# A recurrent attention and feed-forward kernel: reordering the load-and-multiply setup and spreading the feed-forward weight loads over the first steps

## The chip, the cores and the metric

The kernel runs on one core of one Trainium2 chip. The metric is the device time of one execution in microseconds (us), the median of several. Engines: PE is TensorE, DVE is VectorE, ACT is ScalarE, POOL is GpSimd, SP is the engine whose queue issues most of the loads.

## The reference

Two layers with the same weights are applied, each one attention block and one feed-forward block. Attention walks over 64 segments of 32 tokens, one after the other; each segment also sees 8 memory rows that the segment before it produced.

```python
x = x + A(layernorm(x));  x = x + B(layernorm(x))      # twice, same weights

def A(x, mem, Wq, Wk, Wv, Wo):          # 16 heads of 256, model width 448
    for s in range(64):                 # each segment needs the one before
        h = concat(mem, x[32*s : 32*s+32])              # 40 rows
        q, k, v = h @ Wq, h @ Wk, h @ Wv                # per head
        p = softmax(where(mask, q @ k.T / 16, -1e9))
        o = concat_heads(p @ v) @ Wo
        mem, out = o[:8], o[8:]

def B(x):                               # 448 -> 1792 -> 448
    g = x @ W_gate
    return (relu(g) * (x @ W_up)) @ W_down
```

## The kernel before

The kernel never computes q, k and v. In a setup stage it multiplies the weights with each other, per head: M = Wk·Wq (used for the scores) and B = Wv·Wo (used for the values). Then it runs 70 steps; in each, layer 1 handles one segment and layer 2 the segment six steps behind. The feed-forward work is filled into the steps from step 4 on.

K, Q and V arrive through a DMA that transposes on the way. One load of K, Q or V brings 1024 columns, which is four heads, 0.92 MB.

```python
def load_T(n, i):
    t = bp.tile([P, 8, DM], BF, tag=f"w{n}", name=f"w{n}")        # two buffers of each
    nc.sync.dma_start_transpose(t[:], srcs[n][:, 1024 * i:1024 * (i + 1)])
    return t

for i in range(4):                       # M: four groups of four heads
    wk, wq = load_T("k", i), load_T("q", i)
    for hh in range(4):
        for mt in range(3):
            product(ps[:, 0:DM], wk, wq, hh, 128 * mt, 128)       # 2 matmuls of 448 columns
            store_M(...)                                          # copies on ACT and DVE in turn
    ...
nc.sync.dma_start(x_ring[:, 1:R, :], ...)
for i in range(4):                       # B: four groups of four heads
    wv = load_T("v", i)
    nc.sync.dma_start(wo[:], WoF[:, 8 * i:8 * (i + 1), :])
    ...                                                           # same products and copies
nc.sync.dma_start(Wd_sb[:], B_W_down...)                          # 1.6 MB, first used in step 4
...
for half, w in zip(HALVES, (B_W_gate, B_W_up)):                   # 3.2 MB, first used in step 4
    nc.sync.dma_start(Wgu[half], w.rearrange("(c p) n -> p c n", p=64))
```

Only PE's instructions are pinned to program order, and only after the setup. The order of the load queue and of DVE is left to the scheduler. A step, cut to what matters:

```python
def step(g, inG, mid, before, late, end, last):
    # gps: 28 tiles of M x h for even and odd heads, evicted to G by ACT and DVE
    # S_ps: scores = h x G;  mid(): feed-forward work as filler
    vm.both(True)          # values of the memory and of part of the rows, tail rows of B
    # scores -> max, exp (ACT), sum, reciprocal, weights Px / Pm (DVE)
    vm.both(False)         # values, the other rows of B; here PE hides the softmax
    turn_P()               # transposes of the weights on PE
    # AT_ps: weights x values -> mb -> new memory rows (mps) into hTr: the next step waits for these
    nc.sync.dma_start(ys[...], mb[...])       # y<-mb: output rows to where layer 1 adds them up
```

Of the kernel before, what the change touches and what calls it, by code (L numbers as in the profile page):

```python
# [9 lines left out]
BF = mybir.dt.bfloat16  # L10
# [40 lines left out]
def build_kernel(ctx, tc, A_x, A_mem0, A_Wq, A_Wk, A_Wv, A_Wo, B_W_gate, B_W_up, B_W_down, out,  # L51
# [12 lines left out]
    nc.sync.dma_start(x_ring[:, 0, :], x_dram[0:128])  # L64
# [17 lines left out]
    Wd_sb = glob.tile([P, FT, DM], BF)  # L82
# [25 lines left out]
    with tc.tile_pool(name="bpre", bufs=2) as bp:  # L108
        maskf = bp.tile([P, L], F32, bufs=1)
        nc.gpsimd.memset(maskf[:], 0.0)  # L110
        nc.gpsimd.affine_select(
            out=maskf[0:SEG, 0:SEG], in_=maskf[0:SEG, 0:SEG],
            compare_op=ALU.is_ge, fill=MASKVAL, base=0,
            pattern=[[-1, SEG]], channel_multiplier=1,
        )
        nc.vector.memset(maskb[:], 0.0)
        for half in HALVES:
            nc.vector.tensor_copy(maskb[half], maskf[LO].unsqueeze(1).to_broadcast([64, 8, L]))

        srcs = {n: w.rearrange("d h e -> d (h e)") for n, w in (("k", A_Wk), ("q", A_Wq), ("v", A_Wv))}  # L120
        WoF = A_Wo.rearrange("h (t p) d -> p (h t) d", p=P)

        def load_T(n, i):
            t = bp.tile([P, 8, DM], BF, tag=f"w{n}", name=f"w{n}")
            nc.sync.dma_start_transpose(t[:], srcs[n][:, 1024 * i:1024 * (i + 1)])  # L125
            return t

        flip = [0]

        def copy_out(dst, src):  # L130
            flip[0] ^= 1
            if flip[0]:
                nc.scalar.copy(dst, src)
            else:
                nc.vector.tensor_copy(dst, src)

        def product(dst, lt, rt, hh, lo, n):
            for t in range(2):
                nc.tensor.matmul(dst, lt[:, 2 * hh + t, lo:lo + n], rt[:, 2 * hh + t, :],  # L139
                                 start=(t == 0), stop=(t == 1))  # L140

        def store_M(dst, odd, ps):
            if not odd:
                copy_out(dst[:, 0:448], ps)
            else:
                copy_out(dst[:, 512:896], ps[:, 0:384])
                copy_out(dst[:, 448:512], ps[:, 384:448])

        for i in range(4):
            wk = load_T("k", i)  # L150
            wq = load_T("q", i)
            for hh in range(4):
                o = 896 * ((4 * i + hh) // 2)
                for mt in range(3):
                    ps = psum.tile([P, 512], F32, tag="ps")
                    product(ps[:, 0:DM], wk, wq, hh, 128 * mt, 128)
                    store_M(M_sb[:, mt, o:o + 896], hh % 2, ps[:, 0:DM])
            for e in range(2):
                ps = psum.tile([P, 512], F32, tag="ps")
                for side in range(2):  # L160
                    product(ps[64 * side:64 * side + 64, 0:DM], wk, wq, 2 * side + e, 384, 64)
                store_M(MT_sb[:, 896 * i:896 * i + 896], e, ps[:, 0:DM])
        if R > 1:
            nc.sync.dma_start(x_ring[:, 1:R, :], x_dram[128:R * 128].rearrange("(t p) d -> p t d", p=P))
        for i in range(4):
            wv = load_T("v", i)
            wo = bp.tile([P, 8, DM], BF, tag="wo", name="wo")
            nc.sync.dma_start(wo[:], WoF[:, 8 * i:8 * (i + 1), :])
            for hh in range(4):
# [46 lines left out]
    for q in PTs:  # L216
        nc.gpsimd.memset(q[:], 0.0)
# [369 lines left out]
    def none():  # L587
        pass
# [120 lines left out]
```

## Time and profile before

| | before |
|---|---|
| median of 5 runs | 1640.02 us (1639.82 to 1641.61) |
| setup, until step 0's first `gps` matmul | 80.28 us, PE busy 51.51 us |
| step 0 | 25.39 us |
| steps 1 and 2 | 15.25 and 15.83 us |

The page's overview cuts the span into 40 equal slices of about 41 us and gives for each the busy share in tenths. The DMA row is the mean busy share of the 16 DMA engines.

```profile
PE   5778999999999999999999999999999999999997
...
PEclk8989999999999999999999999999999999999999
DMA  9830000000000000000000000000000000000000
```

PE is the bound from the fifth slice on. Only in the first four slices is PE partly idle (besides the very end), above all in the first three, and the DMA engines are 80% busy or more in the first two of them and nearly unused from the fourth on. So the setup and step 0 are the place to look at. The next view is the stage table. Each line is: stretch, its length, busy us and instruction count of PE, PEld (weight loads), DVE, ACT and POOL, then granted clock, DMA share and GB/s.

```profile
core 0: us, PE busy (x) PEld busy (x) DVE busy (x) ACT busy (x) POOL busy (x), PEclk, DMA share, GB/s
0.00:80.28 80.28, 51.51 (x269) 23.65 (x270) 40.34 (x90) 31.92 (x72) 6.04 (x23) 0.89 0.95 212
80.28:105.67 25.39, 17.98 (x397) 12.06 (x397) 9.05 (x22) 5.74 (x14) 3.57 (x8) 0.80 0.65 128
105.67:120.92 15.25, 12.64 (x336) 9.58 (x336) 7.04 (x17) 4.47 (x11) 0.45 (x2) 1.00 0.02 5
120.92:136.75 15.83, 14.91 (x396) 10.64 (x396) 7.91 (x18) 5.19 (x13) 0.45 (x2) 1.00 0.02 5
```

Two facts stand out. In setup the DMA engines are 0.95 busy and PE only 64%. Step 0 does the same work as step 2 and takes 9.6 us longer. The timeline of PE tells where it stands still (start, duration, engine, line, operation, operands, count, and in brackets the idle time before it and what ended it):

```profile
11.18 7.49 PE L139 MATMUL ps<-wq,wk 128*128 128x448 bf16 x32 [11.18 <-DMA wq<-in_A_Wq_dram]
...
33.65 13.72 PE L139 MATMUL ps<-wq,wk 128*128 128x448 bf16 x64 [8.39 <-DMA wq<-in_A_Wq_dram]
...
66.42 12.71 PE L139 MATMUL ps<-wo,wv 128*128 128x448 bf16 x64 [6.56 <-DMA wo<-in_A_Wo_dram]
80.28 0.57 PE L193 MATMUL gps<-hTr,MT_sb 64*128 64x40 bf16 x32 [0.41 <-DVE hTr L260]
90.44 0.45 PE L193 MATMUL gps<-hTr,MT_sb 64*128 64x40 bf16 x16 [5.06 <-issue]
```

Three long waits in setup end with a weight load. The last line is different: for 5.06 us PE waits for nothing that the profile names ("issue"). The DMA view of the six microseconds before 87 us, and then of the one microsecond that follows, gives a hint. Its lines are: queue, kind, packets, MB, share of the 16 engines.

```profile
q1 hardware_dynamic: 350, 1.25, 98.9%
```

```profile
q1 hardware_dynamic: 52, 0.19, 97.8%
q8 instruction: 1, 0.02, 8.7%
```

From 81 to 87 us the gate and up weights fill the engines and not one packet of instructions comes through. Between 87 and 88 us one begins. In the trace this packet holds 16,384 bytes and takes from 87.5 to 88.9 us, and PE goes on at 90.4.

### The profile page before, as it was taken

How to read it: one execution, taken by the hardware profiler on the slowest of the kernel's cores; microseconds unless marked ns; L12 is line 12 of the kernel's file. 1: busy time of each engine (PE TensorE's matmuls, PEld its weight loads, DVE VectorE, ACT ScalarE, POOL GpSimd, SP SyncE). 2: the span in 40 equal slices, each digit the busy share in tenths (PEclk: the TensorE clock that was granted, in tenths of full speed). 3: DMA queues.
4: the chain of work that ended last, by engine and by line, in shares of the span. 5: the costliest groups of instructions: out<-in, count | busy, mean ns of one | idle time of the engine just before them, and what ended most of it. 6: DMA issues, size and time to landing. Idle time of an engine off the chain costs nothing.

```text
span 1638.1 us, 82234 instructions
## 1 busy us (share of the span) xinstructions
PE 1566.3 (96%) x38680; PEld 1176.4 (72%) x38680; DVE 946.0 (58%) x2074; ACT 634.4 (39%) x1430; POOL 140.3 (9%) x370
## 2 busy tenths in 40 slices
PE   5778999999999999999999999999999999999997
PEld 2356767777777777777777777777778777777775
DVE  4634556565566665655656666665655666555553
ACT  2522333444334343434434443434334443434342
POOL 1000011000011010100101100010010100000000
PEclk8989999999999999999999999999999999999999
DMA  9830000000000000000000000000000000000000
GB/s 219 202 78 5 5 6 6 7 5 12 7 11 7 10 7 11 7 6 11 6 12 6 11 6 12 7 8 10 4 12 7 8 7 7 6 9 6 7 5 9
DMA packets 61348, 32.12 MB, mean 20 GB/s; under 512 B 46024, under 2 KB 60112, under 8 KB 61008
## 3 DMA queue, kind: packets, MB, share of 16 engines
q1 hardware_dynamic: 60976, 26.85, 7.1%
q8 instruction: 302, 4.95, 1.3%
q14 instruction: 38, 0.31, 0.1%
q10 hardware_dynamic: 32, 0.01, 0.0%
HBM read 10.33 MB, written 1.84 MB: 7 GB/s over the span
## 4 chain that ended last, share of the span: by engine, by line
PE 83%; DVE 9%; DMA 3%; SPq 2%; issue 1%; POOL 1%; ACT 1%; POOLq 0%; DVEq 0%; ACTq 0%
PE gps L193 27%; PE vps L193 23%; PE gate L193 10%; PE AT_ps L193 7%; PE S_ps L193 6%; PE dps L193 5%; PE PT_ps L196 2%; SPq L125 2%; PE ps L139 1%; DVE Px L471 1%; PE tps L196 1%; DMA y<-mb 1%; DVE ssum L463 1%; DVE vox L353 1%; DVE se L459 1%
## 5 line engine op out<-in xcount | busy, mean ns | idle before, releaser
L193 PE MATMUL gps<-hTr,M_sb 128*128 128x80 bf16 (+1 forms) x11760 | 418.2, 198 | 0.2
L193 PEld LDWEIGHTS <-M_sb 128*128 128x128 bf16 x11760 | 406.3, 99 | 5.0 <-issue 0.5
L401 DVE CAST G<-gps 128x480 bf16<-128x480 f32 (+3 forms) x326 | 190.7, 611 | 218.5 <-PE gps L193 217.7
L193 PEld LDWEIGHTS <-hTr 128*32 128x32 bf16 (+3 forms) x7936 | 197.8, 96 | 147.6 <-issue 40.7
L401 ACT CAST G<-gps 128x480 bf16<-128x480 f32 (+3 forms) x326 | 165.5, 526 | 339.9 <-PE gps L193 339.9
L193 PE MATMUL vps<-B_sb,hTr 128*32 128x448 bf16 x4608 | 242.6, 354 | 0.0
L193 PE MATMUL gate<-xnT,Wgu 64*128 64x128 bf16 x3136 | 206.4, 218 | 1.0 <-ACT xnT L278 1.0
L193 PE MATMUL up<-xnT,Wgu 64*128 64x128 bf16 x3136 | 206.9, 218 | 0.3 <-issue 0.3
L193 PEld LDWEIGHTS <-Wgu 64*128 64x128 bf16 x6272 | 185.2, 95 | 19.5 <-issue 12.7
L193 PE MATMUL vps<-B_sb,memTp 128*32 128x448 bf16 x3360 | 171.7, 353 | 0.0
L353 ACT CAST vox<-vps 128x448 bf16<-128x448 f32 x192 | 99.3, 533 | 175.1 <-PE vps L193 175.1
L353 ACT CAST VOm<-vps 128x448 bf16<-128x448 f32 x210 | 103.5, 526 | 144.2 <-PE vps L193 144.1
L193 PEld LDWEIGHTS <-memTp 128*32 128x32 bf16 (+1 forms) x4480 | 98.4, 95 | 80.0 <-issue 2.2
L353 DVE CAST vox<-vps 128x448 bf16<-128x448 f32 x192 | 116.9, 622 | 56.3 <-PE vps L193 55.2
L291 DVE SCALAR_TENSOR_TENSOR hh<-gate,ut 128x256 bf16<-128x256 f32 x224 | 94.7, 423 | 74.1 <-ACT ut L290 71.4
L193 PEld LDWEIGHTS <-PT 128*64 128x64 bf16 x2048 | 96.9, 110 | 40.2 <-issue 13.7
L290 ACT CAST ut<-up 128x256 bf16<-128x256 f32 x224 | 83.3, 372 | 101.1 <-PE up L193 78.7
L193 PE MATMUL AT_ps<-VOm,PT 128*64 128x320 bf16 (+1 forms) x1280 | 98.4, 262 | 1.3 <-DVE PT L503 1.3
L193 PE MATMUL gps<-hTr,MT_sb 64*128 64x80 bf16 (+1 forms) x3920 | 91.1, 195 | 8.1 <-issue 5.1
L458 DVE TENSOR_REDUCE mx<-S_ps 104x8 f32<-104x320 f32 (+1 forms) x140 | 62.2, 486 | 60.3 <-PE S_ps L193 60.3
L193 PE MATMUL dps<-Wd_sb,hh 128*128 128x448 bf16 x448 | 92.6, 353 | 0.0
L193 PEld LDWEIGHTS <-MT_sb 64*128 64x128 bf16 x3920 | 76.3, 96 | 18.5 <-issue 12.5
(83 smaller groups left out, 1420.9 us busy)
## 6 DMA issues: line engine op xcount, KB each, us to landing
wo<-in_A_Wo_dram SPq DMA_DIRECT2D x4, 896.0 KB, 6.1
y<-mb SPq DMA_DIRECT2D x128, 28.0 KB, 1.8
out_dram<-x_ring SPq DMA_DIRECT2D x16, 112.0 KB, 1.7
Wd_sb<-in_B_W_down_dram SPq DMA_DIRECT2D x1, 1568.0 KB
Wgu<-in_B_W_gate_dram SPq DMA_DIRECT2D x1, 1568.0 KB, 11.8
Wgu<-in_B_W_up_dram SPq DMA_DIRECT2D x1, 1568.0 KB, 18.2
x_ring<-in_A_x_dram SPq DMA_DIRECT2D x11, 112.0 KB, 2.1
x_ring<-in_A_x_dram SPq DMA_DIRECT2D x1, 560.0 KB, 5.1
```

Of the source, the lines that this page charges most:

```text
L125: nc.sync.dma_start_transpose(t[:], srcs[n][:, 1024 * i:1024 * (i + 1)])
L139: nc.tensor.matmul(dst, lt[:, 2 * hh + t, lo:lo + n], rt[:, 2 * hh + t, :], start=(t == 0), stop=(t == 1))
L193: in_order(nc.tensor.matmul(*a, **k))
L196: in_order(nc.tensor.transpose(*a))
L290: nc.scalar.copy(ut[:], gu[1][:])
L291: nc.vector.scalar_tensor_tensor(out=self.hh[:, f:f + 2, :], in0=gu[0][:], scalar=0.0, in1=ut[:], op0=ALU.max, op1=ALU.mult)
L353: self.evac[2 * x + e](self.dst[:, 2 * e + x, :], self.ps[x][e][:, 0:DM])
L401: (cp_a, cp_v)[self.side](G[:, self.side, self.t0:self.t0 + self.n, c0:c1, :], self.ps[:, 0:self.n * NP].rearrange("p (m c t) -> p m c t", ...
L458: nc.vector.tensor_reduce(mx[RR, e], S3, axis=AX.X, op=ALU.max)
L459: nc.vector.tensor_tensor(se[RR, 8 * e:8 * e + 8], S3, mx[RR, e].unsqueeze(2).to_broadcast([nr, 8, L]), op=ALU.subtract)
L463: nc.vector.tensor_reduce(ssum[RR, :], se[RR], axis=AX.X, op=ALU.add)
L471: eng.tensor_tensor(dst, se[rr, :, lo:hi], rs[rr, :].unsqueeze(2).to_broadcast([n, H, hi - lo]), op=ALU.mult)
```

## The change: its intent and the diff

The intent is to keep PE supplied during setup and to take everything out of setup that step 0 does not need. The core of the diff:

```diff
+        # in_order: one chain for each engine, used for the load queue and DVE's setup copies too
-        if pe_last[0] is not None:
-            tc.add_manual_dep(op.ins, pe_last[0], ...)
-        pe_last[0] = op.ins.name
+        eng = op.ins.engine
+        if eng in last_of:
+            tc.add_manual_dep(op.ins, last_of[eng], ...)
+        last_of[eng] = op.ins.name
...
+    def load_vo(j):                       # two heads at a time, V as it lies in memory
+        if j >= 6: ...                    # the last two pairs: V by the transposing DMA, as before
+        w, cols = wvn[j % 2], slice(512 * j, 512 * j + 512)
+        in_order(nc.sync.dma_start(w[:, 0:3, :], srcs["v"][0:384, cols].rearrange("(c p) e -> p c e", p=P)))
+        in_order(nc.sync.dma_start(w[LO, 3, :], srcs["v"][384:448, cols]))
+        in_order(nc.sync.dma_start(wo[:], WoF[:, 4 * j:4 * (j + 1), :]))
...
+    def turn_B(j):                        # 16 transposes on PE, copies of 128x896 on ACT and DVE
+    def mul_B(j):                         # the products of two heads
+    def make_B(j): turn_B(j); mul_B(j)
...
+    load_vo(0); load_vo(1); load_kq(0)
+    make_B(0); load_vo(2); make_B(1); load_vo(3); load_kq(1)
+    make_M(0); load_kq(2)
+    ...                                   # memory rows, first two x tiles
+    for j in (2, 3): make_B(j); load_vo(j + 2)
+    make_M(1); load_kq(3); make_M(2)
+    for j in (4, 5): make_B(j); load_vo(j + 2)
+    ...                                   # other x tiles
+    make_M(3)
...
+        if g == 0:                        # step 0 takes the last two products
+            def mid():  mul_B(6)
+            def soft(): mul_B(7); late_pools()
...
+    # late_pools: gate and up weights in 14 pieces, Wd in 7 (224 KB each), queued in `loads`
+    def load_when(op):                    # issue the next piece once op is done
+        if loads:
+            dma = nc.sync.dma_start(*loads.popleft())
+            tc.add_manual_dep(dma.ins, op.ins.name, ...)
+    # called at DVE's evictions of G, at both exponentials and at both copies of PT
```

More of the change, by code (lines that the diff above doesn't have):

```diff
@@ L63, in build_kernel @@
     x_ring = glob.tile([P, R, DM], BF)
-    nc.sync.dma_start(x_ring[:, 0, :], x_dram[0:128])
+    nc.sync.dma_start(x_ring[:, 0:2, :], x_dram[0:256].rearrange("(t p) d -> p t d", p=P))
     def xsl(t):
@@ L81, in build_kernel @@
     BT_sb = glob.tile([P, H // 2, DM], BF)
-    Wd_sb = glob.tile([P, FT, DM], BF)
     hTr = glob.tile([P, NR, NSL, 2, L], BF)
@@ L106, in build_kernel @@
     psum = ctx.enter_context(tc.tile_pool(name="psum", bufs=8, space=bass.MemoryType.PSUM))
-    with tc.tile_pool(name="bpre", bufs=2) as bp:
-        maskf = bp.tile([P, L], F32, bufs=1)
-        nc.gpsimd.memset(maskf[:], 0.0)
-        nc.gpsimd.affine_select(
-            out=maskf[0:SEG, 0:SEG], in_=maskf[0:SEG, 0:SEG],
-            compare_op=ALU.is_ge, fill=MASKVAL, base=0,
-            pattern=[[-1, SEG]], channel_multiplier=1,
-        )
-        nc.vector.memset(maskb[:], 0.0)
-        for half in HALVES:
-            nc.vector.tensor_copy(maskb[half], maskf[LO].unsqueeze(1).to_broadcast([64, 8, L]))
-        srcs = {n: w.rearrange("d h e -> d (h e)") for n, w in (("k", A_Wk), ("q", A_Wq), ("v", A_Wv))}
-        WoF = A_Wo.rearrange("h (t p) d -> p (h t) d", p=P)
-        def load_T(n, i):
-            t = bp.tile([P, 8, DM], BF, tag=f"w{n}", name=f"w{n}")
-            nc.sync.dma_start_transpose(t[:], srcs[n][:, 1024 * i:1024 * (i + 1)])
-            return t
-        flip = [0]
-        def copy_out(dst, src):
-            flip[0] ^= 1
-            if flip[0]:
-                nc.scalar.copy(dst, src)
-            else:
-                nc.vector.tensor_copy(dst, src)
-        def product(dst, lt, rt, hh, lo, n):
-            for t in range(2):
-                nc.tensor.matmul(dst, lt[:, 2 * hh + t, lo:lo + n], rt[:, 2 * hh + t, :],
-                                 start=(t == 0), stop=(t == 1))
-        def store_M(dst, odd, ps):
-            if not odd:
-                copy_out(dst[:, 0:448], ps)
-            else:
-                copy_out(dst[:, 512:896], ps[:, 0:384])
-                copy_out(dst[:, 448:512], ps[:, 384:448])
-        for i in range(4):
-            wk = load_T("k", i)
-            wq = load_T("q", i)
-            for hh in range(4):
-                o = 896 * ((4 * i + hh) // 2)
-                for mt in range(3):
-                    ps = psum.tile([P, 512], F32, tag="ps")
-                    product(ps[:, 0:DM], wk, wq, hh, 128 * mt, 128)
-                    store_M(M_sb[:, mt, o:o + 896], hh % 2, ps[:, 0:DM])
-            for e in range(2):
-                ps = psum.tile([P, 512], F32, tag="ps")
-                for side in range(2):
-                    product(ps[64 * side:64 * side + 64, 0:DM], wk, wq, 2 * side + e, 384, 64)
-                store_M(MT_sb[:, 896 * i:896 * i + 896], e, ps[:, 0:DM])
-        if R > 1:
-            nc.sync.dma_start(x_ring[:, 1:R, :], x_dram[128:R * 128].rearrange("(t p) d -> p t d", p=P))
-        for i in range(4):
-            wv = load_T("v", i)
-            wo = bp.tile([P, 8, DM], BF, tag="wo", name="wo")
-            nc.sync.dma_start(wo[:], WoF[:, 8 * i:8 * (i + 1), :])
-            for hh in range(4):
-                h = 4 * i + hh
-                for mt in range(3):
-                    ps = psum.tile([P, 512], F32, tag="ps")
-                    product(ps[:, 0:DM], wv, wo, hh, 128 * mt, 128)
-                    copy_out(B_sb[:, mt, place(h), :], ps[:, 0:DM])
-            for pair in range(2):
-                ps = psum.tile([P, 512], F32, tag="ps")
-                for e, half in enumerate(HALVES):
-                    product(ps[half, 0:DM], wv, wo, 2 * pair + e, 384, 64)
-                copy_out(BT_sb[:, place(4 * i + 2 * pair), :], ps[:, 0:DM])
-        nc.sync.dma_start(Wd_sb[:], B_W_down.rearrange("(f p) d -> p f d", p=P))
@@ L182, in build_kernel @@
-    pe_last = [None]
+    last_of = {}
     def in_order(op):
-        if pe_last[0] is not None:
-            tc.add_manual_dep(op.ins, pe_last[0],
+        eng = op.ins.engine
+        if eng in last_of:
+            tc.add_manual_dep(op.ins, last_of[eng],
                               mybir.DependencyInfo(mybir.DependencyClass.NoSync, mybir.DependencyReason.DATA),
                               reason="in_order")
-        pe_last[0] = op.ins.name
+        last_of[eng] = op.ins.name
     def matmul(*a, **k):
@@ L196, in transpose @@
         in_order(nc.tensor.transpose(*a))
-    pa = ctx.enter_context(tc.tile_pool(name="pa", bufs=1))
     p_vo = ctx.enter_context(tc.tile_pool(name="p_vo", bufs=1))
     p_soft = ctx.enter_context(tc.tile_pool(name="p_soft", bufs=1))
-    p_fb = ctx.enter_context(tc.tile_pool(name="p_fb", bufs=2))
-    p_y = ctx.enter_context(tc.tile_pool(name="p_y", bufs=2))
-    Wgu = pa.tile([P, NCH, F], BF)
-    for half, w in zip(HALVES, (B_W_gate, B_W_up)):
-        nc.sync.dma_start(Wgu[half], w.rearrange("(c p) n -> p c n", p=64))
+    p_pp = ctx.enter_context(tc.tile_pool(name="p_pp", bufs=1))
     PXM = []
     for i in range(2):
-        pp = [pa.tile([P, H, SEG], BF, name=f"P{n}{i}") for n in "xm"]
+        pp = [p_pp.tile([P, H, SEG], BF, name=f"P{n}{i}") for n in "xm"]
         for q in pp:
@@ L213, in build_kernel @@
         PXM.append(pp)
-    xnTs = [pa.tile([P, NCH, P], BF, name=f"xnT{i}") for i in range(2)]
-    PTs = [pa.tile([P, 8, P], BF, name=f"PT{i}") for i in range(2)]
+    PTs = [p_pp.tile([P, 8, P], BF, name=f"PT{i}") for i in range(2)]
     for q in PTs:
         nc.gpsimd.memset(q[:], 0.0)
+    bpre = ExitStack()
+    bp = bpre.enter_context(tc.tile_pool(name="bpre", bufs=2))
+    wvn = [bp.tile([P, NSL, 512], BF, name=f"wvn{i}", bufs=1) for i in range(2)]
+    for w in wvn:
+        nc.vector.memset(w[HI, 3], 0.0)
@@ new lines, in build_kernel @@
+    maskf = bp.tile([P, L], F32, bufs=1)
+    nc.gpsimd.memset(maskf[:], 0.0)
+    nc.gpsimd.affine_select(
+        out=maskf[0:SEG, 0:SEG], in_=maskf[0:SEG, 0:SEG],
+        compare_op=ALU.is_ge, fill=MASKVAL, base=0,
+        pattern=[[-1, SEG]], channel_multiplier=1,
+    )
+    nc.vector.memset(maskb[:], 0.0)
+    for half in HALVES:
+        nc.vector.tensor_copy(maskb[half], maskf[LO].unsqueeze(1).to_broadcast([64, 8, L]))
+    srcs = {n: w.rearrange("d h e -> d (h e)") for n, w in (("k", A_Wk), ("q", A_Wq), ("v", A_Wv))}
@@ new lines, in build_kernel, with load_T, load_kq @@
+    WoF = A_Wo.rearrange("h (t p) d -> p (h t) d", p=P)
+    def load_T(n, i):
+        t = bp.tile([P, 8, DM], BF, tag=f"w{n}", name=f"w{n}")
+        in_order(nc.sync.dma_start_transpose(t[:], srcs[n][:, 1024 * i:1024 * (i + 1)]))
+        return t
+    kq, vo, turned = {}, {}, {}
+    def load_kq(i):
+        kq[i] = load_T("k", i), load_T("q", i)
+    def load_vo(j):
+        if j >= 6:
+            if j == 6:
+                kq["v"] = bp.tile([P, 8, DM], BF, tag="wk", name="wk")
+                in_order(nc.sync.dma_start_transpose(kq["v"][:], srcs["v"][:, 3072:4096]))
+            wo = bp.tile([P, 4, DM], BF, tag="wo", name="wo")
+            in_order(nc.sync.dma_start(wo[:], WoF[:, 4 * j:4 * (j + 1), :]))
+            turned[j] = kq["v"][:, 4 * (j - 6):4 * (j - 6) + 4], wo
+            return
+        w, cols = wvn[j % 2], slice(512 * j, 512 * j + 512)
+        in_order(nc.sync.dma_start(w[:, 0:3, :], srcs["v"][0:384, cols].rearrange("(c p) e -> p c e", p=P)))
+        in_order(nc.sync.dma_start(w[LO, 3, :], srcs["v"][384:448, cols]))
+        wo = bp.tile([P, 4, DM], BF, tag="wo", name="wo")
+        in_order(nc.sync.dma_start(wo[:], WoF[:, 4 * j:4 * (j + 1), :]))
+        vo[j] = w, wo
@@ new lines, in build_kernel, with copy_out, product, store_M @@
+    flip = [0]
+    def copy_out(dst, src):
+        flip[0] ^= 1
+        if flip[0]:
+            nc.scalar.copy(dst, src)
+        else:
+            in_order(nc.vector.tensor_copy(dst, src))
+    def product(dst, lt, rt, hh, lo, n):
+        for t in range(2):
+            matmul(dst, lt[:, 2 * hh + t, lo:lo + n], rt[:, 2 * hh + t, :], start=(t == 0), stop=(t == 1))
+    def store_M(dst, odd, ps):
+        if not odd:
+            copy_out(dst[:, 0:448], ps)
+        else:
+            copy_out(dst[:, 512:896], ps[:, 0:384])
+            copy_out(dst[:, 448:512], ps[:, 384:448])
@@ new lines, in make_M @@
+    def make_M(i):
+        wk, wq = kq.pop(i)
+        for hh in range(4):
+            o = 896 * ((4 * i + hh) // 2)
+            for mt in range(3):
+                ps = psum.tile([P, 512], F32, tag="ps")
+                product(ps[:, 0:DM], wk, wq, hh, 128 * mt, 128)
+                store_M(M_sb[:, mt, o:o + 896], hh % 2, ps[:, 0:DM])
+        for e in range(2):
+            ps = psum.tile([P, 512], F32, tag="ps")
+            for side in range(2):
+                product(ps[64 * side:64 * side + 64, 0:DM], wk, wq, 2 * side + e, 384, 64)
+            store_M(MT_sb[:, 896 * i:896 * i + 896], e, ps[:, 0:DM])
@@ new lines, in make_B @@
+    def make_B(j):
+        turn_B(j)
+        mul_B(j)
+    def turn_B(j):
+        wn, wo = vo.pop(j)
+        wv = bp.tile([P, 4, DM], BF, tag="wv", name="wv")
+        for a in range(2):
+            tp = psum.tile([P, 2, 512], BF, tag="ps", name="tp")
+            for b in range(2):
+                for dc in range(NSL):
+                    transpose(tp[:, b, 128 * dc:128 * dc + 128],
+                              wn[:, dc, 128 * (2 * a + b):128 * (2 * a + b) + 128], ident[:])
+            copy_out(wv[:, 2 * a:2 * a + 2, :], tp[:, :, 0:DM])
+        turned[j] = wv, wo
@@ new lines, in mul_B @@
+    def mul_B(j):
+        wv, wo = turned.pop(j)
+        ps = psum.tile([P, 512], F32, tag="ps")
+        for e, half in enumerate(HALVES):
+            product(ps[half, 0:DM], wv, wo, e, 384, 64)
+        copy_out(BT_sb[:, place(2 * j), :], ps[:, 0:DM])
+        for hh in range(2):
+            for mt in range(3):
+                ps = psum.tile([P, 512], F32, tag="ps")
+                product(ps[:, 0:DM], wv, wo, hh, 128 * mt, 128)
+                copy_out(B_sb[:, mt, place(2 * j + hh), :], ps[:, 0:DM])
@@ L222, in ln @@
         stats = p_ln.tile([P, nc.vector.BN_STATS_DIM], F32, tag="ln_stats")
-        nc.vector.bn_stats(stats[:], xt)
+        (in_order if t >= 2 else (lambda op: None))(nc.vector.bn_stats(stats[:], xt))
         mv = p_ln.tile([P, nc.vector.BN_AGGR_DIM], F32, tag="ln_mv")
@@ L275, in turn @@
                 transpose(tps[:, k], self.xn[:, k].rearrange("p a b -> p (a b)"), ident[:])
-            self.xnT = xnTs[n_xn[1] % 2]
+            self.xnT = late_sb["xnT"][n_xn[1] % 2]
             n_xn[1] += 1
             nc.scalar.copy(self.xnT[:], tps[:])
-            self.hh = p_fb.tile([P, FT, P], BF, tag="hh", name="hh")
+            self.hh = late_sb["fb"].tile([P, FT, P], BF, tag="hh", name="hh")
         def gate_up(self, f):
@@ L286, in gate_up @@
                     for half, ps in zip(HALVES, gu):
-                        matmul(ps[:, ff], Wgu[half, k, col], self.xnT[half, k],
+                        matmul(ps[:, ff], late_sb["Wgu"][half, k, col], self.xnT[half, k],
                                          start=(k == 0), stop=(k == NCH - 1))
-            ut = p_fb.tile([P, 2, P], BF, tag="ut")
+            ut = late_sb["fb"].tile([P, 2, P], BF, tag="ut")
             nc.scalar.copy(ut[:], gu[1][:])
@@ L298, in down @@
             for f in range(lo, hi):
-                matmul(ps[:, 0:DM], self.hh[:, f, :], Wd_sb[:, f, :], start=(f == 0), stop=(f == FT - 1))
+                matmul(ps[:, 0:DM], self.hh[:, f, :], late_sb["Wd"][:, f, :], start=(f == 0), stop=(f == FT - 1))
             if hi < FT:
@@ L357, in both, with late_pools @@
             self.part(1, tail)
+    late_sb = {}
+    ys = {}
+    loads = deque()
+    def late_pools():
+        bpre.close()
+        pa = ctx.enter_context(tc.tile_pool(name="pa", bufs=1))
+        late_sb["fb"] = ctx.enter_context(tc.tile_pool(name="p_fb", bufs=2))
+        late_sb["y"] = ctx.enter_context(tc.tile_pool(name="p_y", bufs=2))
+        late_sb["xnT"] = [pa.tile([P, NCH, P], BF, name=f"xnT{i}") for i in range(2)]
+        Wgu = late_sb["Wgu"] = pa.tile([P, NCH, F], BF, name="Wgu")
+        Wd = late_sb["Wd"] = pa.tile([P, FT, DM], BF, name="Wd")
+        for k in range(NCH):
+            for half, w in zip(HALVES, (B_W_gate, B_W_up)):
+                loads.append((Wgu[half, k], w[64 * k:64 * k + 64, :]))
+        for f in range(0, FT, 2):
+            loads.append((Wd[:, f:f + 2, :], B_W_down[128 * f:128 * f + 256, :].rearrange("(f p) d -> p f d", p=P)))
+    def load_when(op):
+        if loads:
+            dma = nc.sync.dma_start(*loads.popleft())
+            tc.add_manual_dep(dma.ins, op.ins.name,
+                              mybir.DependencyInfo(mybir.DependencyClass.Sync, mybir.DependencyReason.DATA),
+                              reason="load_when")
     prev_vom = [None]
@@ L361, in build_kernel, with step @@
     cp_v = nc.vector.tensor_copy
-    def step(g, inG, mid, before, late, end, last):
+    def step(g, inG, mid, soft, before, late, end, last):
         chains = [c for c in (C1, C2) if 0 <= g - c.lag < nseg]
@@ L400, in out @@
             def out(self):
-                (cp_a, cp_v)[self.side](
+                op = (cp_a, cp_v)[self.side](
                     G[:, self.side, self.t0:self.t0 + self.n, c0:c1, :],
                     self.ps[:, 0:self.n * NP].rearrange("p (m c t) -> p m c t", m=self.n, t=L))
+                if self.side:
+                    load_when(op)
         def pair_of_banks(k):
@@ L438, in step @@
         vm = Values(lambda rr, k: memTp[g % 2][rr, k, :], VOm, [cp_a, cp_v, cp_a, cp_a])
-        vm.both(True)
+        if g:
+            vm.both(True)
         for c in chains:
@@ L460, in step @@
                                     mx[RR, e].unsqueeze(2).to_broadcast([nr, 8, L]), op=ALU.subtract)
-            nc.scalar.activation(se[RR, 8 * e:8 * e + 8], se[RR, 8 * e:8 * e + 8], AF.Exp, scale=SCALE)
+            load_when(nc.scalar.activation(se[RR, 8 * e:8 * e + 8], se[RR, 8 * e:8 * e + 8], AF.Exp, scale=SCALE))
         ssum = p_soft.tile([P, H], F32, tag="ssum")
@@ L502, in turn_P @@
                     transpose(PT_ps[:, g4, RR], Pt[RR, 4 * g4:4 * g4 + 4, :], ident[RR, RR])
-                cp(PT[:, gg:gg + 4, RR], PT_ps[:, :, RR])
+                load_when(cp(PT[:, gg:gg + 4, RR], PT_ps[:, :, RR]))
             late()
+        soft()
+        if not g:
+            vm.both(True)
         vm.both(False)
@@ L562, in step @@
             if j == 0:
-                ys[c.cid] = p_y.tile([P, DM], BF, tag=f"y{c.cid}", name="y")
+                ys[c.cid] = late_sb["y"].tile([P, DM], BF, tag=f"y{c.cid}", name="y")
             nc.sync.dma_start(ys[c.cid][32 * j:32 * j + 32, :], mb[c.rb:c.rb + SEG, 0:DM])
@@ L567, in step @@
         last()
-    ys = {}
     xn_of = {}
@@ L578, in prep_pe, with none @@
             prep_x(c, t, xn_of.pop((c.cid, t)))
+    def none():
+        pass
+    load_vo(0)
+    load_vo(1)
+    load_kq(0)
+    make_B(0)
+    load_vo(2)
+    make_B(1)
+    load_vo(3)
+    load_kq(1)
+    make_M(0)
+    load_kq(2)
     tps0 = transposed(mem_in, MEM)
@@ L585, in build_kernel @@
         prep_pe(C1, t)
-    def none():
-        pass
+    for j in (2, 3):
+        make_B(j)
+        load_vo(j + 2)
+    make_M(1)
+    load_kq(3)
+    make_M(2)
+    for j in (4, 5):
+        make_B(j)
+        load_vo(j + 2)
+    if R > 2:
+        in_order(nc.sync.dma_start(x_ring[:, 2:R, :], x_dram[256:R * 128].rearrange("(t p) d -> p t d", p=P)))
+    make_M(3)
     nc.gpsimd.tensor_copy(memTp[0][:, :, 0:16], hTr[:, 1, :, 0, 0:16])
@@ L594, in build_kernel, with mid, soft, end @@
             set_mem0(C2)
-        inG = mid = before = late = end = last = none
-        if r == 0:
+        inG = mid = soft = before = late = end = last = none
+        if g == 0:
+            def mid():
+                mul_B(6)
+            def soft():
+                mul_B(7)
+                late_pools()
+            def end():
+                prep_ln(C1, gb + 2)
+        elif r == 0:
             def inG():
@@ L647, in last @@
                 fill(1, 1)
-        step(g, inG, mid, before, late, end, last)
+        step(g, inG, mid, soft, before, late, end, last)
         for c in (C1, C2):
```

## The prediction

> **What bounds it now.** Overall TensorE: the page has PE at 96% of the span, and the chain of waits is 83% PE. The steady part (192.7 to 1600 us, PE 98.8% busy) is barely touched; the change concerns the first 106 us. The stage table gives: setup 0 to 80.28 us, PE busy 51.5 us, DMA share 0.95; step 0 from 80.28 to 105.67, that is 25.4 us, where steps 1 and 2 take 15.3 and 15.8 us.
>
> In setup PE stands still for about 28 us (timeline): 11.2 us for the first turned weights, 8.4 us (25.3 to 33.6) for the third pair, 6.5 us (60 to 66.4) for a Wo, and 2 us in small waits. Three times it then runs at half speed for about 4 us (matmuls 0.375 us apart, not 0.19), losing about 2 us each. [...] In step 0 PE waits 5.06 us at 85.4 for "issue" while the 3.1 MB of gate and up weights pour in (landing 11.8 and 18.2 us, DMA share above 1.0). I take that for instruction fetch behind the load.
>
> **What changes.** Three quarters of V is read plainly, not by transposing DMA (3.7 to 7.4 us of queue time each), and turned on PE; PE starts with V·Wo products, before K and Q have come; the queue is held in program order; Wd and Wgu come in 21 pieces of about 229 KB in steps 0 to 3; the last two of eight value products move into step 0.
>
> **Costs.** At full clock one M group (4 heads) takes about 5.8 us of PE and one two-head value product about 2.75 us. New per turned pair of heads: 16 transposes, 1.25 us (8 took 0.62), and about 1.3 us waiting for the last 128x896 copy (that form takes 0.905 us on ACT). So 5.3 us each, six of them 32 us; four M groups 23 us; memory and x transposes 1.2 us; start at about 6.5 us (1.15 MB at the 300 to 380 GB/s that plain loads showed at 50 to 58 us); one half-clock start 2 us. Sum: step 0 begins at about 65 us, 15 us earlier. By my queue schedule (4 us per transposing load) K/Q groups land at about 15, 30, 38 and 53 us, each before PE wants it: PE-bound, little slack.
>
> Step 0: without the wait and its half-clock tail about 16 us, plus two value products (5.5 us): about 21.5, so 4 us won. Steps 1 to 3 and the rest unchanged (the DMA is 2% busy there); all the gain is critical, since every step waits for the one before.
>
> **Prediction: 1620 us**, 1.2% faster; 1610 to 1630 holds it 8 times in 10. Faster by over 2%: 0.07; within 2%: 0.92; slower: 0.01.
>
> **Right if:** step 0's first gps matmul at 60 to 69 us; the first PE work at 6 to 8 us; no PE wait over 3 us on DMA in setup; no 5 us issue wait in step 0; step 0 at 20 to 23 us; steps 1 to 3 within 0.5 us of before; from the first feed-forward on the same length within 3 us.
>
> **Wrong if:** in-order queue waits starve PE (a K/Q group comes late, PE cools again); the small plain rows (0.9 to 1 KB) are slow; the spread pieces delay instruction fetch in several steps; or DVE/ACT order shifts in the steady part (7 us per half per cent of 1400).

## The result, and the profile after

| | before | after |
|---|---|---|
| median of the runs made side by side | 1640.02 us (13 runs) | 1619.28 us (7 runs, 1617.53 to 1621.16) |
| step 0's first `gps` matmul | 80.28 us | 61.38 us |
| step 1's first `gps` matmul | 105.67 us | 82.83 us |
| memory rows of step 5 into `hTr` (before layer 2 begins) | 192.47 us | 168.96 us |
| end of the profiled span | 1638.1 us | 1616.5 us |

The ratio is 0.987, with a 95% interval of 0.986 to 0.988. (Ratios are the mean time of one kernel's fast runs over that of the other's of the same rounds, so not quite the ratio of the medians.) The change is 1.3% faster. The overview of the page after:

```profile
PE   7988999999999999999999999999999999999997
...
PEclk9999999999999999999999999999999999999999
DMA  9630000000000000000000000000000000000000
```

The first three slices of PE have gone from 5, 7, 7 to 7, 9, 8. The stage table after, at the same boundaries of the work:

```profile
0.00:61.36 61.36, 50.98 (x332) 26.33 (x332) 38.79 (x88) 33.73 (x70) 8.29 (x27) 1.00 1.05 245
61.36:82.83 21.47, 20.40 (x431) 13.06 (x430) 13.60 (x31) 9.45 (x21) 1.03 (x3) 1.00 0.14 42
82.83:97.81 14.98, 12.47 (x336) 9.51 (x336) 7.03 (x17) 4.47 (x11) 0.45 (x2) 1.00 0.43 111
97.81:113.70 15.89, 14.97 (x396) 10.69 (x396) 7.90 (x18) 5.19 (x13) 0.45 (x2) 1.00 0.39 107
```

Setup is 18.9 us shorter, and PE is busy 83% of it. (The DMA share of 1.05 is above 1: the packets' times, added up, exceed the span of the 16 engines, so some of them overlap.) Step 0 is 3.9 us shorter although it now holds two value products. Steps 1 and 2 keep their lengths while their DMA share rises from 0.02 to 0.43 and 0.39: the feed-forward weights now come in there. The timeline of PE after:

```profile
4.75 0.50 PE L122 MATMUL tp<-ident,wvn 128*128 128x128 bf16 x3 [4.75 <-DMA wvn<-in_A_Wv_dram]
6.75 1.55 PE L122 MATMUL tp<-ident,wvn 128*128 128x128 bf16 x13 [1.50 <-DMA wvn<-in_A_Wv_dram]
...
40.90 5.58 PE L119 MATMUL ps<-wq,wk 128*128 128x448 bf16 x32 [1.37 <-DMA wq<-in_A_Wq_dram]
...
82.83 0.57 PE L119 MATMUL gps<-hTr,MT_sb 64*128 64x40 bf16 x32 [0.28 <-DVE hTr L612]
```

PE works from 4.75 us on, and after its start it waits for a load only once, 1.37 us. The 5 us wait for issue is gone.

**The rest of the span.** I compared the moment at which each step's memory rows of layer 1 are copied to `hTr`. The difference between the kernels is 22.84 us after step 0 and 23.51 us after step 5. Most of the 63 steps agree to 0.02 us. About a dozen, half of them the first of a group of four, differ by 0.2 to 1.9 us, in both directions, and by the end the difference is 21.6 us. The largest is step 44. There layer 1's rows are written to `y` by a DMA and added to x before the feed-forward can start. The timeline of DVE after, and then of the same addition before:

```profile
1030.83 0.39 DVE L626 TENSOR_TENSOR x_ring<-y,x_ring 128x448 bf16<-128x448 bf16 x1 [2.66 <-DMA y<-mb]
```

```profile
1053.12 0.39 DVE L566 TENSOR_TENSOR x_ring<-y,x_ring 128x448 bf16<-128x448 bf16 x1 [0.78 <-DMA y<-mb]
```

In the kernel after, DVE happened to wait 1.9 us longer for the landing of that small transfer, and the step is 1.87 us longer. The other differing steps were not looked at one by one. Whole times of one kernel scatter by some 1 to 8 us between executions; that such landings are the reason is likely, but not shown. The moments in the first 200 us compare kernels more sharply than the medians do, though each comes from one execution.

### The profile page after: what moved, and what is told of

Same layout as the page of the kernel before. It is cut to its first block, busy times and chain, and to the rows that moved or that the text cites. A ratio compares the mean times of both kernels' runs of the same rounds, so it can differ in the third digit from the quotient of the medians.

```text
span 1616.5 us, 82492 instructions
## 1 busy us (share of the span) xinstructions
PE 1566.7 (97%) x38776; PEld 1178.6 (73%) x38776; DVE 948.9 (59%) x2082; ACT 639.8 (40%) x1436; POOL 140.1 (9%) x370
## 4 chain that ended last, share of the span: by engine, by line
PE 84%; DVE 10%; DMA 2%; issue 1%; POOL 1%; ACT 1%; SPq 0%; POOLq 0%; DVEq 0%; ACTq 0%
PE gps L119 27%; PE vps L119 23%; PE gate L119 10%; PE AT_ps L119 7%; PE S_ps L119 6%; PE dps L119 5%; PE ps L119 3%; PE PT_ps L122 2%; DMA y<-mb 2%; DVE Px L528 1%; DVE vox L380 1%; PE tps L122 1%; DVE ssum L520 1%; DVE se L516 1%; DVE stats L250 1%
## 5 line engine op out<-in xcount | busy, mean ns | idle before, releaser
L317 ACT CAST ut<-up 128x256 bf16<-128x256 f32 x224 | 83.3, 372 | 99.4 <-PE up L119 77.8
L515 DVE TENSOR_REDUCE mx<-S_ps 104x8 f32<-104x320 f32 (+1 forms) x140 | 62.3, 486 | 58.8 <-PE S_ps L119 58.8
L119 PE MATMUL dps<-Wd,hh 128*128 128x448 bf16 x448 | 92.6, 353 | 0.0
L119 PE MATMUL S_ps<-G,hTr 128*40 128x160 bf16 (+1 forms) x1792 | 88.1, 245 | 0.7
```

What stands on the lines that cost most here:

```text
L119: in_order(nc.tensor.matmul(*a, **k))
L317: nc.scalar.copy(ut[:], gu[1][:])
L515: nc.vector.tensor_reduce(mx[RR, e], S3, axis=AX.X, op=ALU.max)
```

## The experiments

The table gathers the moments of every run, in us, read from the timelines and from the spans. The paragraphs after it use them.

| run | step 0 begins | step 1 begins | step 5's memory rows | end of span | median |
|---|---|---|---|---|---|
| before | 80.28 | 105.67 | 192.47 | 1638.1 | 1640.02 |
| after | 61.38 | 82.83 | 168.96 | 1616.5 | 1619.28 |
| e1_before_spread | 78.71 | 94.60 | 180.60 | 1627.4 | 1629.00 |
| e2_after_bulk | 60.60 | 83.39 | 176.54 | 1622.3 | 1623.76 |
| e3_after_vturn | 64.37 | 85.81 | 173.59 | 1620.9 | 1622.30 |
| e4_before_order | 85.57 | 109.60 | 196.13 | 1641.9 | 1644.01 |
| e5_after_unmoved | 68.11 | 84.32 | 170.67 | 1617.1 | 1618.74 |
| e6_after_ahead | 61.21 | 83.75 | 169.37 | 1615.5 | 1618.06 |
| e8_before_late | 74.20 | 90.10 | 175.81 | 1625.8 | 1627.20 |
| e9_after_kqfirst | 64.58 | 86.02 | 173.12 | 1619.1 | 1620.52 |
| e10_one_q | 56.19 | 77.65 | 165.24 | 1611.6 | 1612.28 |

Each median of an experiment is of 4 runs. The first four experiments ran together on one chip (before there: 1640.83 us), then e5, e6, e8 and e9 together (before: 1638.93 us), then e10 (before: 1639.15 us).

How far can a moment of a single execution be trusted? Some runs have the same setup program, so their setups show the scatter. e2 and e5 equal the kernel after up to the fourth K/Q group, whose products begin at 55.86 us (after), 55.08 (e2) and 56.95 (e5); before the third group PE waits 1.37 us for Q in the kernel after, 1.79 in e5, and not for a load at all in e2. e1 has the setup of the kernel before, and begins step 0 1.6 us earlier. Differences of less than about 2 us before step 0 are thus not shown by one trace each.

### e1: the spread loads alone

```diff
 # in the kernel before
-    for half, w in zip(HALVES, (B_W_gate, B_W_up)):
-        nc.sync.dma_start(Wgu[half], w.rearrange("(c p) n -> p c n", p=64))
+    loads = deque()
+    for k in range(NCH):
+        for half, w in zip(HALVES, (B_W_gate, B_W_up)):
+            loads.append((Wgu[half, k], w[64 * k:64 * k + 64, :]))
+    # load_when() as in the kernel after, at the same places of the step
```

> The kernel before, only the gate and up weights split into 14 pieces, each issued when an eviction, exponential or PT copy of steps 0 and 1 is done. Theory (PE's 5.06 us issue wait in step 0 is instruction fetch behind the 3.1 MB bulk load): the wait falls under 1 us, the half-clock tail after it goes too, step 0 falls from 25.4 us to 18 to 19 us, the total by 6 to 7 us to about 1633.5. Rival (the wait belongs to entering the step code or to a semaphore, not to the load): step 0 stays at 25 us, the total at 1640.

Measured: 1629.00 us, ratio 0.9936 (0.992 to 0.9952). The stage table's line of step 0, from its first matmul to that of step 1:

```profile
78.71:94.60 15.89, 14.91 (x396) 10.64 (x396) 8.48 (x21) 5.62 (x13) 3.10 (x7) 1.00 0.36 104
```

The wait for issue has fallen below 1 us, the granted clock is 1.00 where it was 0.80, and step 0 takes 15.9 us instead of 25.4. So the theory holds in kind, and the size was more than I wrote: 9.5 us in step 0, not 6 to 7. The stall of 5.06 us cost nearly twice its length, because matmuls after it ran at half clock (granted 0.50 from 90.4 to 93.6 us in the kernel before) and other small waits went too (the one of 1.60 us for `vox` at 99.4 us among them). A further 1.6 us lies before step 0, which the edit does not touch; the loads of setup landed somewhat earlier in this run. I count it as scatter between executions.

### e2: the bulk load put back into the kernel after

```diff
-        for k in range(NCH):
-            for half, w in zip(HALVES, (B_W_gate, B_W_up)):
-                loads.append((Wgu[half, k], w[64 * k:64 * k + 64, :]))
-        for f in range(0, FT, 2):
-            loads.append((Wd[:, f:f + 2, :], ...))
+        for half, w in zip(HALVES, (B_W_gate, B_W_up)):
+            loads.append((Wgu[half], w.rearrange("(c p) n -> p c n", p=64)))
+        loads.append((Wd[:], B_W_down.rearrange("(f p) d -> p f d", p=P)))
```

> The kernel after, with the feed-forward weights in three whole loads (gate, up, Wd: 4.7 MB), released by the last copies of step 0 and the first eviction of step 1. Theory (fetch behind a bulk load): an issue wait of 4 to 6 us on PE appears in step 1 and perhaps again in step 2, followed by half-clock matmuls; the total rises by 5 to 10 us to 1624 to 1629. Rival (the wait was tied to the first entry into the step code): steps 1 and 2 keep 15.0 and 15.9 us, total 1619.

Measured: 1623.76 us, ratio to before 0.9903 (0.9878 to 0.9928). The timeline of PE in step 1, and the stage table's line of step 1:

```profile
94.38 0.94 PE L119 MATMUL vps<-BT_sb,memTp 64*32 64x448 bf16 x15 [5.28 <-issue]
```

```profile
83.39:105.28 21.89, 14.42 (x336) 10.33 (x336) 7.13 (x17) 4.47 (x11) 0.45 (x2) 0.84 0.90 199
```

The stall follows the load. It now stands in step 1, at another instruction, is as long (5.28 us), and step 1 takes 21.9 us instead of 15.0. Step 5's memory rows come 7.6 us later than in the kernel after; the median rises by 4.5 us, just under the 5 to 10 expected. In the trace a 16 KB instruction packet runs from 91.4 to 92.8 us; PE goes on at 94.4. The rival, that entering the step code was to blame, is out.

The packets of the instruction queue q8 tie the stall to the fetch. In step 0 the first of them begins 2.0 us after the step's first matmul in e1 and 7.3 us after it in the kernel before: 5.2 us later, beside a stall of 5.06. In step 1 it begins 2.7 us after the first matmul in the kernel after and 8.1 us after it in e2: 5.3 us later, beside a stall of 5.28. e4, below, keeps the bulk load and is a third case: its packet begins 8.0 us into step 0, and PE stands still for 5.09 us. The same pattern appears in small without the feed-forward weights: in step 0 of e2 and e6 PE waits 1.19 and 0.93 us for issue; there the last loads of setup run until about 63 us, and the packet begins at 63.0 and 63.4 us, against 62.3 in the kernel after, which has no such wait. What stays open is where in the DMA engines the packet waits: no view shows when it was asked for.

### e8: Wd out of setup too

```diff
 # on top of e1
-        nc.sync.dma_start(Wd_sb[:], B_W_down.rearrange("(f p) d -> p f d", p=P))
+    for f in range(0, FT, 2):
+        loads.append((Wd_sb[:, f:f + 2, :], B_W_down[128 * f:128 * f + 256, :]...))
```

> The kernel before with gate and up weights spread (as in the earlier run) and Wd too taken out of setup, in 7 more pieces. Theory (setup of before is bound by the DMA engines, and Wd's 1.6 MB stand in front of the last V and Wo): the 6.5 us wait for the third Wo shrinks by 4 to 6 us, step 0 begins at 73 to 75 us, total 1623 to 1625. Rival (Wd moves in slack): step 0 begins at 78 to 79 us, total 1628 to 1630.

Measured: 1627.20 us, ratio 0.9922 (0.9907 to 0.9937). The timeline of PE:

```profile
60.08 12.52 PE L139 MATMUL ps<-wo,wv 128*128 128x448 bf16 x64 [2.55 <-DMA wo<-in_A_Wo_dram]
...
74.20 0.57 PE L192 MATMUL gps<-hTr,MT_sb 64*128 64x40 bf16 x32 [0.87 <-DVE hTr L267]
```

The wait for the third Wo falls from 6.5 us to 2.55, and step 0 begins at 74.2 us, 4.5 us earlier than in e1. Wd was issued in the middle of setup and took engine time from the loads that PE was waiting for. The total came out 2.2 us above the expected 1623 to 1625, while step 5 is 4.8 us earlier than in e1. Most of the difference was lost again in later steps of this execution, and by whole times e8 and e1 are not told apart: their intervals overlap. What Wd is worth is shown at the wait and at step 5, not in the total.

### e4: program order alone

```diff
 # in the kernel before: in_order() for each engine, on the setup's loads, DVE copies,
 # matmuls and on bn_stats of x tiles from the second on, as in the kernel after
```

> The kernel before, only held to program order on the load queue and on DVE in setup (so the third K/Q pair is no longer queued behind the x tiles and the first V). Theory (order alone is worth the 8.4 us wait): PE's longest setup wait for K/Q falls below 5 us, step 0 begins at about 72 us, total about 1632. Rival (the DMA engines are the bound whatever the order): the wait only moves, to V and Wo at the end; step 0 begins at 78 to 81 us, total 1638 to 1641.

Measured: 1644.01 us, ratio 1.0021 (1.0 to 1.0042). The timeline of PE:

```profile
29.15 8.02 PE L150 MATMUL ps<-wq,wk 128*128 128x448 bf16 x32 [3.95 <-DMA wq<-in_A_Wq_dram]
...
63.30 5.58 PE L150 MATMUL ps<-wo,wv 128*128 128x448 bf16 x32 [3.44 <-DMA wo<-in_A_Wo_dram]
71.81 7.18 PE L150 MATMUL ps<-wo,wv 128*128 128x448 bf16 x32 [2.93 <-DMA wo<-in_A_Wo_dram]
84.75 0.89 PE L198 MATMUL tps<-ident,xn 128*128 128x128 bf16 x4 [5.25 <-DVE xn L239]
```

The wait for the third K/Q pair shrinks from 8.4 to 3.95 us, as both sides had it, but waits of 3 to 4 us for V and Wo come up instead. The last 5.25 us are a flaw of my edit: it holds the second tile's layer norm behind all copies of setup. Even without them step 0 would, by this estimate, begin at about 80.3 us (85.57 minus 5.25), no earlier than before. So program order on its own, with K and Q first, is worth nothing that these traces show, and the 8.4 us wait was not a mistake of order that could simply be put right: the loads as a whole did not come faster.

### e3: V by the transposing DMA, in the new order

```diff
 # in the kernel after
-        in_order(nc.sync.dma_start(w[:, 0:3, :], srcs["v"][0:384, cols]...))
-        in_order(nc.sync.dma_start(w[LO, 3, :], srcs["v"][384:448, cols]))
+        wv = bp.tile([P, 4, DM], BF, tag="wv", name="wv")
+        in_order(nc.sync.dma_start_transpose(wv[:], srcs["v"][:, 512 * j:512 * j + 512]))
 ...
     def make_B(j):
-        turn_B(j)
         mul_B(j)
```

> The kernel after, with all of V turned by the transposing DMA as before (512 columns at a time), so that PE turns nothing; queue order, start with V and Wo, spread loads and moved products kept. Prediction's theory (plain V pays because the transposing DMA is the slow part): step 0 begins at 70 us or later, total 1628 or more. Rival 1 (the order of the queue and the smaller first pieces are the gain; plain V trades about 10 us of PE work for DMA time): step 0 begins at 61 to 67 us, total 1619 to 1625. Rival 2 (setup is bound by PE alone): step 0 begins by 55 us, total 1613 or less.

Measured: 1622.30 us, ratio to before 0.9895 (0.9871 to 0.9919). The timeline of PE:

```profile
19.62 7.26 PE L119 MATMUL ps<-wq,wk 128*128 128x448 bf16 x32 [2.90 <-DMA wq<-in_A_Wq_dram]
...
58.85 5.58 PE L119 MATMUL ps<-wq,wk 128*128 128x448 bf16 x32 [2.46 <-DMA wq<-in_A_Wq_dram]
64.37 0.57 PE L119 MATMUL gps<-hTr,MT_sb 64*128 64x40 bf16 x32
```

Step 0 begins at 64.4 us, 3.0 us later than in the kernel after, in the range of the first rival. PE has 96 transposes and their copy waits less to do, and yet it is later: each of the four K/Q groups now waits 2.2 to 2.9 us for its load. Loading V plainly is thus worth about 3 us of the 18.9 by this one trace, not most of it. It buys DMA time with PE time. The whole times do not separate the two kernels: the intervals of their ratios overlap.

### e5: the last two products back in setup

```diff
     make_M(3)
+    mul_B(6)
+    mul_B(7)
 ...
-            def mid():
-                mul_B(6)
             def soft():
-                mul_B(7)
                 late_pools()
```

> The kernel after, with the last two value products put back before step 0. Theory (step 0 is 95% PE busy, so the moved work costs PE the same there, 5.8 us for two): step 0 begins 5.5 to 6 us later, at about 67, is 5.5 to 6 us shorter, about 15.7 us, and the total stays within 1.5 us of the kernel after. Rival (the move hides the products in waits of step 0): step 0 shortens by less than 3 us and the total rises by 3 to 6 us.

Measured: 1618.74 us, ratio to before 0.9867 (0.9849 to 0.9885). The stage table's line of step 0:

```profile
68.11:84.32 16.21, 14.82 (x398) 10.63 (x398) 9.72 (x23) 5.38 (x13) 1.03 (x3) 1.00 0.12 31
```

Step 0 begins 6.7 us later and is 5.3 us shorter, and its PE time falls by 5.6 us (20.40 to 14.82). Step 1 begins 1.5 us later than in the kernel after, but 1.1 of these are there already at the fourth K/Q group (56.95 against 55.86 us), where the two programs do not yet differ. Moving the products to step 0 mainly carries the same PE work to another place. The rival, that they hide in waits, is out.

### e6: the turns issued ahead

```diff
-    def make_M(i):
+    def make_M(i, amid=()):
 ...
+        for j in amid:                    # before the last products of the group
+            turn_B(j)
 ...
-    make_M(0)
+    make_M(0, (2, 3))
 ...
-        make_B(j)                          # for j in (2, 3) and in (4, 5)
+        mul_B(j)
 ...
-    make_M(2)
+    make_M(2, (4, 5))
```

> The kernel after, with the PE transposes of pairs 2 to 5 put before the last products of an M group, so that PE no longer waits 0.9 us for the copy of each turned pair (four waits, some 3.6 us in all). Prediction's theory (setup is PE-bound): step 0 begins 3 to 4 us earlier, at 57.5 to 58.5, total about 1615.5. Rival (the DMA engines, over 1.0 busy by the stage table from 3 to 62 us, are as close a bound): PE waits longer for K/Q instead, step 0 begins 0 to 1.5 us earlier, total 1618 to 1619.

Measured: 1618.06 us, ratio to before 0.9873 (0.9853 to 0.9892). The timeline of PE:

```profile
33.97 5.58 PE L119 MATMUL ps<-wq,wk 128*128 128x448 bf16 x32 [2.01 <-DMA wq<-in_A_Wq_dram]
...
41.13 4.70 PE L119 MATMUL ps<-wq,wk 128*128 128x448 bf16 x24 [1.58 <-DMA wq<-in_A_Wq_dram]
...
55.70 5.58 PE L119 MATMUL ps<-wq,wk 128*128 128x448 bf16 x32 [0.83 <-DMA wq<-in_A_Wq_dram]
...
61.21 0.57 PE L119 MATMUL gps<-hTr,MT_sb 64*128 64x40 bf16 x32
```

Of PE's waits for the copies of these four pairs one is left (0.54 us), and step 0 begins where it did (61.21 against 61.38 us), outside the 57.5 to 58.5 expected by more than the scatter. The waits came back as 4.4 us of waits for K/Q, where the kernel after has 1.4. So setup of the kernel after is not bound by PE alone. The median is not distinguishable from the kernel after's.

### e10: the same PE work with less to load

```diff
 # on top of e6; wrong results on purpose
-        kq[i] = load_T("k", i), load_T("q", i)
+        wk = load_T("k", i)
+        if i == 0:
+            kq["q"] = bp.tile([P, 8, DM], BF, name="wq_only", bufs=1)
+            in_order(nc.sync.dma_start_transpose(kq["q"][:], srcs["q"][:, 0:1024]))
+        kq[i] = wk, kq["q"]
```

> The kernel after with the PE transposes ahead (as in the earlier run), and only the first of the four Q loads done, its data used for all four M groups: wrong results on purpose, the same PE work, 2.75 MB less to load (three transposing loads of some 3.9 us of queue time). Theory (with the turns ahead, what holds setup is the arrival of K/Q, by DMA): the K/Q waits (4.4 us in the run before this) go and step 0 begins at 56 to 58 us, so PE's own bound is about 57. Rival (something else than DMA holds setup at 61, evictions on DVE and ACT for instance): step 0 begins at 60 to 61.5 us.

Measured: 1612.28 us, ratio to before 0.9832 (0.9815 to 0.9848). The timeline of PE has no wait for K or Q left, and this line:

```profile
56.19 0.57 PE L119 MATMUL gps<-hTr,MT_sb 64*128 64x40 bf16 x32
```

Step 0 begins 5.0 us earlier than in e6. The arrival of the loads is what held e6. With most of the waiting for loads out of the way PE needs about 56 us, so in e6 the two bounds lie within some 5 us of each other. Lighter loads without the turns ahead were not run. (The comparison with the reference passed although the scores used the wrong Q; with these inputs the tolerance does not notice it. The run is of no use as a kernel.)

### e9: K and Q first

```diff
+    load_kq(0)
     load_vo(0)
     load_vo(1)
-    load_kq(0)
+    make_M(0)
+    load_kq(1)
     make_B(0)
     ...
     load_vo(3)
-    load_kq(1)
-    make_M(0)
     load_kq(2)
```

> The kernel after, with the first K/Q pair loaded and multiplied before the first two V/Wo pairs. Theory (setup bound by DMA in its sum): PE starts at about 11 instead of 6.8 us and yet step 0 begins within 2 us of 61.4, total 1618 to 1621. Rival (PE-bound: each us of a later start is carried to the end): step 0 begins at 65 to 67, total 1623 to 1625.

Measured: 1620.52 us, ratio to before 0.9886 (0.9872 to 0.9901). The timeline of PE:

```profile
10.81 8.19 PE L119 MATMUL ps<-wq,wk 128*128 128x448 bf16 x32 [10.81 <-DMA wq<-in_A_Wq_dram]
```

PE begins 4 to 6 us later, and step 0 begins at 64.58 us, 3.2 us later. That is just outside of both expectations, between the two pure bounds; the median lies in the first one's range. After its start PE waits for no load at all in this run, so from 10.8 us on the end is set by PE's own work and its waits for copies. Part of the late start is made up because the 1.37 us wait for Q of the kernel after is absent. It fits a setup in which PE and the DMA engines are both nearly full, but it does not prove it.

## Why the prediction was right, and where it was not

**The total.** Predicted 1620 us (1610 to 1630), measured 1619.28. That the two lie within 1 us is partly luck: up to step 1 the kernel won 22.8 us and not the 19 of the sum, and some 2 us were lost again in single later steps and in the scatter. The path to it:

- **Step 0's start was predicted at about 65 us (range 60 to 69) and is 61.38.** The sum was made of PE's pieces, and these came out as follows. PE's first long stretch begins at 6.75 us (predicted 6.5); three transposes run at 4.75 us already, so the sign "first PE work at 6 to 8 us" was missed. The first pair takes 6.9 us with the half-speed start (predicted 5.3 + 2; its matmuls come 0.373 us apart until 12.5 us, later ones 0.189). The next five pairs take 4.7 us on average instead of 5.3: 16 transposes took 1.06 us rather than 1.25, the products 2.9 us (e6: 5.83 for two pairs) rather than 2.75, which leaves about 0.8 us of waiting for the copies rather than 1.3. The four M groups take 5.6 us rather than 5.8. One wait of 1.37 us for Q is added (it varies between executions, see above). The term that was mis-sized is the turned pair, by about 3 us in five.
- **Step 0 was predicted at 21.5 us and takes 21.47**: 16 us without the stall (e1 measured 15.9) and two products at 5.5 us (e5 measured 5.6 us of PE).
- **"The 5 us wait is instruction fetch behind the load"** was argued from one line of the profile. e1 and e2 show that the stall is the bulk load's doing: it goes when the load is spread, and it comes back in another step when the load is made whole again. The first instruction packet of the step comes later by as much as PE stands still (5.2 and 5.3 us), so it is the fetch that the load holds up. In the overall sum I entered the wait as 4 us net, because I set the two moved products against it. Taken alone, the spreading is worth 11.9 us at step 5 (10.3 without the 1.6 us of scatter before step 0), the largest single part of the change, and my expectation for e1 was too small.
- **"PE-bound, with little slack"** is the step of the prediction that failed in part. e6 removes most of PE's waits for copies and gains nothing; e10 removes loads as well and gains 5 us. Setup after the change is held by PE and, close behind, by the loads. My queue schedule had every K/Q group land before PE wanted it; in the profiled execution the third came 1.4 us too late, in e2's, with the same setup, it came in time, in e5's it was 1.8 us late. The forecast sign, no wait over 3 us for a load once PE has started, held.
- **What I did not price at all is Wd leaving the setup.** Built up from PE's pieces, the sum contained it unseen. Added to e1, e8 shows 4.8 us at step 5. I had also read the 8.4 us wait of the kernel before as one that a better order would remove; e4 shows that with the same loads it only moves.
- **Steps 1 to 3 within 0.5 us**: the differences against before are within 0.3 us, while the loads run beside them. **The rest within 3 us**: from step 5 to the end the difference changes by 1.9 us, in single steps that differ both ways.

Where the 23.5 us at step 5 come from, along one path: spreading gate and up weights 11.9 us (before to e1), Wd out of setup 4.8 us (e1 to e8), and everything else, which is the new order with V first, plain V and the moved products, 6.8 us (e8 to after). Seen from the kernel after, undoing plain V costs 4.6 us at step 5, of which 1.3 us arise in step 1, where the first 12 `AT_ps` matmuls took 2.03 us in that execution and the 16 of the kernel after 1.72. Undoing the move costs 1.7 us, most of it scatter of the setup (see e5). These are not additive, since each of them shifts the balance of the two bounds, and the 6.8 us were not divided further.

No run points to a version that is clearly better than the kernel after. e6 equals it within the scatter.

## What to carry to other kernels

Before rearranging work, look at what the loads of a busy stretch are for: here two loads that nothing needed until step 4 cost more than half of what was won (11.9 and 4.8 of 23.5 us at step 5), one by competing with the weights PE waited for and one by standing in the way of PE's own instructions. An idle stretch that ends in "issue" while a bulk load is in flight (here 5.06 us, under 1 us once the load was spread) is best tried by splitting that load and tying its pieces to work as it proceeds. When one bound has been lowered to meet another, price the next step against both: hiding about 3 us of PE waits won nothing while the loads were as heavy, and 5 us came when they were lighter too.

## Further readings of the traces

- The instruction packets of q8 are of 16,384 bytes. Beside a bulk load PE stood still 5.06 us (before) and 5.28 us (e2), and step 0 lost 9.5 us in all (25.4 against 15.9 us in e1).
- A transposing load moved 290 GB/s while it ran (stage table, 66.2 to 68.6 us of the kernel before), and several in a row 224 to 227 GB/s, with the gaps between them (28 to 32 us). Plain loads moved 349 to 381 GB/s (52 to 56 us), and the plain load of the gate and up weights, into 64 partitions, 201 to 226 (82 to 90 us).
- In the kernel before, the granted clock was 0.50 after waits of 8.39, 6.56 and 5.06 us (33.6 to 39.0, 66.4 to 69.7 and 90.4 to 93.6 us), and after the first two of them matmuls of 448 columns came 0.373 us apart instead of 0.189. It was also 0.50 from 100.4 to 103.8 us, soon after a wait of 1.60 us. In e3 an M group took 7.26 us after a wait of 2.90 us and 7.27 after one of 2.34, but 5.58 after waits of 2.20 and 2.46.
- Waits for one 28 KB `y<-mb` transfer of 0.78 and 2.66 us were seen in the same place of two executions, and the step with the later landing was 1.87 us longer.
